# k.v of batches 2 to 7: four 64x64 corners of PE in place of two 64x128 halves

## The chip, the cores and the metric

One core of one Trainium2 chip. The metric is the device time of one execution in microseconds (us). The notes cited as "the Trainium skill" are given with the page's title and section.

Engines: PE (TensorE; PEld is its weight load), DVE (VectorE), ACT (ScalarE), POOL (GpSimd), SP (SyncE).

## The reference

Linear attention on 8 batches of 8 heads, 576 positions, 64 features, followed by a gated feed-forward block on the 4608 rows of 512 that come out.

```python
def _attn_ref(q, k, v):
    phi = lambda x: np.where(x > 0, x, np.exp(x) - 1.0) + 1.0
    q_p, k_p = (phi(q), phi(k))
    kv = np.einsum('bhsd,bhse->bhde', k_p, v)       # 64 x 64 per head: "k.v"
    z = np.sum(k_p, axis=2)
    num = np.einsum('bhsd,bhde->bhse', q_p, kv)
    den = np.einsum('bhsd,bhd->bhs', q_p, z)[..., None] + 1e-06
    return num / den

def _moe_ref(x, w_gate, w_val, w_out):              # 512 -> 1536 -> 512
    g = x @ w_gate
    return (g * (1.0 / (1.0 + np.exp(-g))) * (x @ w_val)) @ w_out
```

## The kernel before

After a start that handles batches 0 and 1 and the first group of 512 rows (g = 0), a main loop of eight iterations, g = 1 to 8, does the feed-forward block of one further group each on PE. In between it prepares attention for batch g + 1, piece by piece: iteration 1 prepares batch 2, iteration 6 prepares batch 7, iterations 7 and 8 prepare no batch. Below is what the change and the argument touch.

A tile of k or v holds two groups of four heads: the even heads on partitions 0 to 63, the odd heads on partitions 64 to 127. `mm1` multiplies 64 positions of two heads of k (128 columns of weights) by the same two heads of v (2 x 65 columns; column 65 of each head is 1, so that it sums k into z). The two halves of the partitions (`hh`) run side by side on the two row halves of PE, into two PSUM banks. Of each 128x129 result only the two 64x64 blocks on the diagonal and one z column are used; the cross products of one head with the other are waste.

```python
def mm1(b, lp):                                   # k.v of two of the four heads per half
    ...
    W = 2 * D + (b > 1)                           # D = 64
    for j in range(J):                            # J = 9 steps of 64 positions
        for hh in range(2):
            rows = slice(C * hh, C * hh + C)      # C = 64
            if b < 2: vv = v16[b][rows, 2 * lp:2 * lp + 2, D * j:D * j + D]
            else:     vv = vm[b % 2][rows, j, :, :].rearrange("p l c -> p (l c)")[:, 130 * lp:130 * lp + W]
            nc.tensor.matmul(out=kvb[b][hh][:, 256 * lp:256 * lp + W],
                             lhsT=kp[b % 2][rows, j, P * lp:P * lp + P], rhs=vv,
                             start=(j == 0), stop=(j == J - 1))

def zdiag(b, lp):                                 # DVE: zd = diagonal matrix of z
    ... nc.vector.tensor_scalar(out=zd[...], in0=id16, scalar1=kvb[b][hh][:, 256 * lp + D:...], ...)

def zb(b):                                        # PE: broadcasts z to all partitions
    nc.tensor.matmul(out=zps[b], lhsT=ones, rhs=zd, start=True, stop=True)

def steady(b, late=0):                            # (n, f): f is issued after the n-th gate pair
    ... (0, phi_q(b, 0)), (1, phi_q(b, 1)), (1, mm1(b, 0)), (1, mm1(b, 1)),
        (2, zdiag(b, 0)), (2, zdiag(b, 1)), (2, r_copies(b)),
        (3 + (late > 0), zb(b)), (3 + (late > 0), zb_copy(b)), (3 + (late > 0), s3_prod(b, 0)),
        (4, s3_reduce(b, 0)), ... (11, s3_recip(b, 2))
```

A "gate pair" n is eight 128x512 matmuls (four into a bank pG, four into a bank pV), then on ACT `sil` = silu of pG, then on DVE `hT` = pV x sil. Iteration 1 is called with `late=2`: all its items come two gate pairs later, and zb one more. In the traces each engine starts this work in program order, so the order of the items is the order on each engine.

## Time and profile before

| | before |
|---|---|
| time, median of the first 4 runs | 331.31 us (330.93 to 331.93) |
| span of the profiled run | 329.4 us |
| PE busy | 317.2 us, 96% |
| k.v of one batch, last full matmul before to first after | 1.44 us |
| iterations 1 to 6, in us | 33.09, 33.36, 33.35, 33.35, 33.32, 33.50 |

An iteration is counted from its first gate matmul to the next one's, in the trace.

The page of the kernel before: busy time by engine, then the granted clock of PE in 40 slices (in tenths of full speed), then the engines' shares in the chain that ended last.

```profile
PE 317.2 (96%) x1957; PEld 150.0 (46%) x1957; DVE 220.0 (67%) x398; ACT 167.6 (51%) x239; POOL 40.5 (12%) x50
...
PEclk9969999999999999999999999999999999999999
...
PE 82%; ACT 5%; DVE 5%; issue 3%; DMA 2%; POOL 1%; SPq 0%; ACTq 0%; POOLq 0%; DVEq 0%
```

PE is busy nearly always, and a first reading is that any PE time saved is time won. The timeline of PE in iteration 2 says otherwise. Columns: start in us, duration in us, engine, line, operation, tiles and shapes.

```profile
98.08 0.38 PE L275 MATMUL pV_115<-xT_0_96,wv 128*128 128x512 f16 x1
98.39 0.23 PE L165 MATMUL pX_118<-vm_76,kp_72 64*128 64x129 f16 x1
98.40 0.23 PE L165 MATMUL pX_119<-vm_76,kp_72 64*128 64x129 f16 x1
98.46 0.22 PE L165 MATMUL pX_118<-vm_76,kp_72 64*128 64x129 f16 x1
98.46 0.22 PE L165 MATMUL pX_119<-vm_76,kp_72 64*128 64x129 f16 x1
...
99.37 0.22 PE L165 MATMUL pX_119<-vm_76,kp_72 64*128 64x129 f16 x1
99.52 0.39 PE L275 MATMUL pG_112<-xT_0_90,wg 128*128 128x512 f16 x1
...
102.77 0.38 PE L275 MATMUL pV_114<-xT_0_96,wv 128*128 128x512 f16 x1
103.16 0.38 PE L195 MATMUL pX_117<-zd,ones 128*128 128x512 f16 x1
```

L165 is k.v: 18 pairs, one pair per 56 ns. L195 is zb. Full matmuls normally start 0.216 us apart, but zb starts 0.386 us after the one before it: it waited 0.17 us, although the durations overlap and PE looks busy. A wait this short does not show as idle time; it shows as a distance between starts. In iterations 2 to 6 that distance is 386, 374, 374, 341 and 523 ns.

What zb waits for is the last zd on DVE. The chain of waits of the kernel before, between 230 and 237 us (iteration 6): start in us, length in us, what.

```profile
230.23 0.10 DVE hT_98 L281
230.33 0.51 issue
230.84 0.46 DVE eq L125
...
233.75 1.12 DVE qp_74 L127 x2
234.87 0.40 issue
235.27 0.69 DVE hT_98 L281
235.96 0.68 DVE zd L171 x4
236.64 0.04 issue
236.68 0.38 PE pX_117 L195
```

The chain to zb runs along DVE: three hT and the phi of q in between, then four zd. k.v is not in it. ("issue" is time in which the engine waited for nothing that the profile shows.)

### The profile page before, as it was taken

The page shows a single profiled execution, that of the slowest core. Times are in us where ns is not written, and L with a number is a line of the kernel's source. Part 1 is how long each engine was busy: PE and PEld are TensorE (multiplying, and loading weights), DVE is VectorE, ACT ScalarE, POOL GpSimd, SP SyncE. Part 2 cuts the span into 40 slices and gives each one's busy share as a digit, 9 for nine tenths or more (in the row PEclk, how much of TensorE's full clock was granted, in tenths as well). Part 3 has the DMA queues.
Part 4 walks back from the last instruction along what each step waited for, and adds up shares of the span by engine and source line. Part 5 has one row for each costly group of instructions (what it writes and reads, how often), then busy time and mean ns, then how long its engine had stood idle before and what let it go on. Part 6 is the DMA issues. An engine that isn't in the chain of part 4 may idle for free.

```text
span 329.4 us, 5083 instructions
## 1 busy us (share of the span) xinstructions
PE 317.2 (96%) x1957; PEld 150.0 (46%) x1957; DVE 220.0 (67%) x398; ACT 167.6 (51%) x239; POOL 40.5 (12%) x50
## 2 busy tenths in 40 slices
PE   8579999999999999999999999999999999999994
PEld 6434454454444444544444444444444444444443
DVE  3855776688978885888588858885887344234321
ACT  3626998927844684458445844584431233123310
POOL 7895410010001000100010000000000000000000
PEclk9969999999999999999999999999999999999999
DMA  7999999999395538363737340224112410140014
GB/s 106 175 125 177 203 207 208 218 225 152 65 159 105 105 80 166 57 115 75 148 71 125 63 100 15 26 54 97 27 24 48 98 32 0 31 91 8 2 32 96
DMA packets 40984, 32.18 MB, mean 98 GB/s; under 512 B 16256, under 2 KB 36480, under 8 KB 40960
## 3 DMA queue, kind: packets, MB, share of 16 engines
q0 software_dynamic: 20640, 18.88, 37.1%
q1 hardware_dynamic: 20160, 12.85, 17.8%
q8 instruction: 15, 0.25, 0.3%
q10 hardware_dynamic: 160, 0.13, 0.2%
q14 instruction: 9, 0.07, 0.1%
HBM read 37.75 MB, written 9.44 MB: 143 GB/s over the span
## 4 chain that ended last, share of the span: by engine, by line
PE 82%; ACT 5%; DVE 5%; issue 3%; DMA 2%; POOL 1%; SPq 0%; ACTq 0%; POOLq 0%; DVEq 0%
PE pG_112 L275 13%; PE pG_113 L275 12%; PE pV_114 L275 8%; PE pV_115 L275 8%; PE pV_116 L275 8%; PE pV_115 L296 7%; PE pG_112 L296 7%; PE pV_114 L296 7%; PE pG_113 L296 6%; DMA q_0_65<-in_q_dram 2%; PE pX_118 L165 2%; DVE hT_98 L281 1%; DVE kp_71 L365 1%; ACT ek L121 1%; ACT sil_100 L280 1%
## 5 line engine op out<-in xcount | busy, mean ns | idle before, releaser
L275 PEld LDWEIGHTS <-wv 128*128 128x128 f16 x432 | 42.5, 98 | 51.6 <-issue 1.1
L275 PEld LDWEIGHTS <-wg 128*128 128x128 f16 x432 | 41.4, 98 | 50.7 <-issue 2.1
L280 ACT ACTIVATE sil_100<-pG_112 128x512 f16<-128x512 f32 x51 | 30.5, 597 | 51.7 <-PE pG_112 L275 45.6
L280 ACT ACTIVATE sil_101<-pG_113 128x512 f16<-128x512 f32 x51 | 30.5, 597 | 37.8 <-PE pG_113 L275 35.1
L296 PEld LDWEIGHTS <-hT_98 128*128 128x128 f16 x228 | 21.4, 98 | 26.0 <-issue 1.5
L296 PEld LDWEIGHTS <-hT_99 128*128 128x128 f16 x192 | 18.4, 98 | 22.8 <-issue 0.9
L306 DVE TENSOR_SCALAR osb_104<-pV_115 128x512 f32<-128x512 f32 x9 | 6.2, 689 | 16.8 <-PE pV_115 L296 16.8
L215 DVE TENSOR_REDUCE den<-prod 128x12 f32<-128x768 f16 x18 | 17.0, 943 | 0.0
L296 PE MATMUL pV_114<-wo,hT_98 128*128 128x512 f16 x60 | 14.1, 379 | 0.2 <-DVE hT_98 L281 0.2
L296 PE MATMUL pV_115<-wo,hT_98 128*128 128x512 f16 x60 | 14.1, 379 | 0.0
L296 PE MATMUL pG_112<-wo,hT_98 128*128 128x512 f16 x60 | 14.1, 379 | 0.0
L281 DVE SCALAR_TENSOR_TENSOR hT_98<-pV_114,sil_100 128x512 f16<-128x512 f32 x11 | 7.6, 691 | 8.4 <-PE pV_114 L275 6.3
L304 ACT ACTIVATE osb_103<-pG_112 128x512 f32<-128x512 f32 x8 | 4.7, 584 | 16.3 <-PE pG_112 L296 16.3
L306 DVE TENSOR_SCALAR osb_105<-pG_113 128x512 f32<-128x512 f32 x8 | 5.5, 691 | 9.4 <-PE pG_113 L296 9.4
L296 PE MATMUL pG_113<-wo,hT_98 128*128 128x512 f16 x48 | 11.4, 380 | 0.0
L296 PE MATMUL pG_113<-wo,hT_99 128*128 128x512 f16 x48 | 11.1, 380 | 0.0
L296 PE MATMUL pV_114<-wo,hT_99 128*128 128x512 f16 x48 | 11.0, 379 | 0.0
L296 PE MATMUL pG_112<-wo,hT_99 128*128 128x512 f16 x48 | 11.0, 379 | 0.0
L296 PE MATMUL pV_115<-wo,hT_99 128*128 128x512 f16 x48 | 11.0, 379 | 0.0
L275 PE MATMUL pG_113<-xT_0_90,wg 128*128 128x512 f16 x27 | 10.5, 388 | 0.0
L275 PE MATMUL pG_113<-xT_0_92,wg 128*128 128x512 f16 x27 | 10.5, 388 | 0.0
L275 PE MATMUL pG_112<-xT_0_90,wg 128*128 128x512 f16 x27 | 10.5, 388 | 0.0
(240 smaller groups left out, 745.2 us busy)
## 6 DMA issues: line engine op xcount, KB each, us to landing
k_1_64<-in_k_dram POOLq DMA_DIRECT2D x4, 576.0 KB, 7.3
q_1_66<-in_q_dram POOLq DMA_DIRECT2D x4, 576.0 KB, 9.4
v_1_68<-in_v_dram POOLq DMA_DIRECT2D x4, 576.0 KB, 11.5
out_dram<-osb_102 SPq DMA_DIRECT2D x18, 128.0 KB, 2.4
out_dram<-osb_103 SPq DMA_DIRECT2D x18, 128.0 KB, 2.4
out_dram<-osb_104 SPq DMA_DIRECT2D x18, 128.0 KB, 2.4
out_dram<-osb_105 SPq DMA_DIRECT2D x16, 128.0 KB, 2.6
k_0_63<-in_k_dram POOLq DMA_DIRECT2D x3, 576.0 KB, 15.8
```

Source lines behind the costliest of these rows:

```text
L121: nc.scalar.activation(out=e[:, s, :], in_=src[b % 2][:, s, :], func=AF.Exp, bias=0.0, scale=1.0)
L165: nc.tensor.matmul(out=kvb[b][hh][:, 256 * lp:256 * lp + W], lhsT=kp[b % 2][rows, j, P * lp:P * lp + P], rhs=vv, start=(j == 0), stop=(j = ...
L215: nc.vector.tensor_reduce(out=den[:, HL * j0:HL * j1], in_=prod[:, 0:j1 - j0, :].rearrange("p j (l d) -> p (j l) d", d=D), axis=AX.X, op=A ...
L275: nc.tensor.matmul(out=ps[:, :], lhsT=src[:, i, P * fb:P * fb + P], rhs=xT[i][g % 2][:, :], start=(i == 0), stop=(i == 3))
L280: nc.scalar.activation(out=s[:, :], in_=pg[:, :], func=AF.Silu, bias=0.0, scale=1.0)
L281: nc.vector.scalar_tensor_tensor(out=hT[g % 2][:, fb, :], in0=pv[:, :], scalar=SC, in1=s[:, :], op0=ALU.mult, op1=ALU.mult)
L296: nc.tensor.matmul(out=pso[(g, t)][:, :], lhsT=hT[g % 2][:, fb, P * t:P * t + P], rhs=wo[:, fb, :], start=(fb == 0), stop=(fb == FB - 1))
L304: nc.scalar.activation(out=o[:, :], in_=ps[:, :], func=AF.Copy, bias=0.0, scale=1.0 / SC)
L306: nc.vector.tensor_scalar(out=o[:, :], in0=ps[:, :], scalar1=1.0 / SC, scalar2=None, op0=ALU.mult)
L365: eng.tensor_scalar(out=dst[:, :, P * lp:P * lp + P].rearrange("p j (s d) -> p s j d", d=D), in0=src[:, 2 * lp:2 * lp + 2, :].rearrange("p ...
```

## The change

The intent is to compute only what is used: one head per 64x64 corner of PE, four corners at once, 65 columns instead of 129. The useless cross products go, and the copy of the result to R reads and writes half as much.

```diff
-    R = two([P, 4, P + 1], FP16, "R")
+    R = two([P, 4, P], FP16, "R")
 ...  def mm1(b, lp):
-                if b < 2: ...  else: vv = vm[b % 2][rows, j, :, :]...[:, 130 * lp:130 * lp + W]
-                nc.tensor.matmul(out=kvb[b][hh][:, 256 * lp:256 * lp + W], lhsT=kp[b % 2][rows, j, P * lp:P * lp + P],
-                                 rhs=vv, start=(j == 0), stop=(j == J - 1))
+                if b < 2: ...  (as before); continue
+                for e in range(2):
+                    nc.tensor.matmul(
+                        out=kvb[b][hh][D * e:D * e + D, 256 * lp:256 * lp + D + 1],
+                        lhsT=kp[b % 2][rows, j, P * lp + D * e:P * lp + D * e + D],
+                        rhs=vm[b % 2][rows, j, 2 * lp + e, :], start=(j == 0), stop=(j == J - 1))
 ...  def r_copies(b):
-        W = 2 * D + (b > 1)
+        W = D
 ...  def kv(b):
-        c1 = D + (b > 1)
+        c1 = D if b < 2 else 0
```

More of the change, by code (lines that the diff above doesn't have):

```diff
@@ L161, in mm1 @@
                 if b < 2:
-                    vv = v16[b][rows, 2 * lp:2 * lp + 2, D * j:D * j + D]
-                else:
-                    vv = vm[b % 2][rows, j, :, :].rearrange("p l c -> p (l c)")[:, 130 * lp:130 * lp + W]
-                nc.tensor.matmul(
-                    out=kvb[b][hh][:, 256 * lp:256 * lp + W], lhsT=kp[b % 2][rows, j, P * lp:P * lp + P], rhs=vv,
-                    start=(j == 0), stop=(j == J - 1))
+                    nc.tensor.matmul(
+                        out=kvb[b][hh][:, 256 * lp:256 * lp + P], lhsT=kp[b % 2][rows, j, P * lp:P * lp + P],
+                        rhs=v16[b][rows, 2 * lp:2 * lp + 2, D * j:D * j + D], start=(j == 0), stop=(j == J - 1))
+                    continue
+                for e in range(2):
+                    nc.tensor.matmul(
+                        out=kvb[b][hh][D * e:D * e + D, 256 * lp:256 * lp + D + 1],
+                        lhsT=kp[b % 2][rows, j, P * lp + D * e:P * lp + D * e + D],
+                        rhs=vm[b % 2][rows, j, 2 * lp + e, :], start=(j == 0), stop=(j == J - 1))
     def zdiag(b, lp):
@@ L175, in r_copies @@
     def r_copies(b):
-        W = 2 * D + (b > 1)
+        W = D
         for hh in range(2):
```

## The prediction

> **What bounds the kernel.** The page gives PE 317.2 of 329.4 us busy (96%); the chain of waits is 82% PE, mostly 128x512 matmuls, one per 0.216 us in the timeline. But PE is not the limit everywhere. In iterations 2 to 6 of the main loop (they prepare batches 3 to 7) the matmul that broadcasts z ("zb", ones x zd) starts late: in the timeline 386, 374, 374, 341 and 523 ns after the matmul before it, against a normal 216. It waits for DVE, which from the iteration's first hT to the last zd runs without a pause (iteration 2: 96.84 to 103.10). The chain of waits for the last such block (230.2 to 236.7 us) runs along DVE, not PE.
>
> **What k.v costs now.** One batch: 18 pairs of row halves, a pair per 56 ns (129 columns), 1.02 us; from the last full matmul before to the first after, 1.44 us (98.08 to 99.52), of which 0.31 is the way into the tiled mode and 0.15 the way out. Six batches.
>
> **What the change does.** 72 matmuls of 64x64 on 65 columns, 18 quartets of corners per batch; twice the instructions. From the trace: pairs on 64 columns (z sums of batch 1, 48.1 to 48.6 us) start every 29 ns. In the existing corner matmuls four start within 10 ns, and a quartet on 64 columns follows another after 28 ns when queued behind longer work (258.97, 259.00), 52 ns when fresh (26.56, 26.62). The Trainium skill, "TensorEngine Tiling (Array Packing)", Restrictions and Gotchas, says that column tiling excludes Fast Weight Load; the trace agrees in kind: 64x64 loads take 103 to 108 ns, 64x128 ones 92 to 95. The 28 ns quartet shows that the slower load still hides. So 52 + 16 x 29 = about 0.52 us for the run: the block shrinks from 1.44 to about 0.96 us. Estimate: 0.48 us less PE time per batch, 2.9 us in all. The copies of kv to R shrink from 258 to 128 columns on ACT (0.39 to about 0.28 us each, estimate from the 512-column evictions at 0.597); ACT is off the chain.
>
> **How much is on the critical path.** k.v lies between the DVE chain's start and zb in iterations 2 to 6. zd there waits not for k.v but for DVE work queued ahead. So PE arrives 0.48 us earlier at zb and waits 0.48 us longer: nothing gained. Only batch 2 (iteration 1), whose zb comes later in the order and waits for nothing (no gap at 75.08), keeps its 0.48 us.
>
> **Predicted: 330.8 us** (331.3 less 0.5), 330.1 to 331.6. Faster by over 2%: 1%; within 2%: 98%; slower by over 2%: 1%.
>
> **What would show it.** Quartets every 29 to 30 ns; the block 1.44 to 0.96 us; the gap before zb grows by 0.48 us in iterations 2 to 6 (to 0.80 to 1.0 us between starts); DVE time from first hT to last zd unchanged at 6.3 to 6.4 us; the iteration that prepares batch 2 0.5 us shorter, the next five unchanged.
>
> **What would make it wrong.** If instructions can't be fed at 8 per 29 ns (the fastest run in the trace is 4 per 29), quartets take up to 56 ns and the gain is nil. If the four weight loads share one port, a quartet costs about 107 ns and the kernel loses up to 5 us, still under 2%. If the DVE chain itself is released by something that moves with k.v, up to 2.9 us are gained (328.4).

## The result, and the profile after

The changed kernel took 330.19 us (median of 4 runs, 329.67 to 330.44), against 331.31 us (median of 4, 330.93 to 331.93). The ratio is 0.9962, with a 95% interval of 0.9943 to 0.9982. A ratio here is the mean time of one kernel's runs over that of the other's of the same rounds, so it is not quite the ratio of the medians that are quoted. The medians differ by 1.1 us, twice the 0.5 that was forecast. Two later comparisons gave 330.19 against 330.94 us (ratio 0.9983) and 330.38 against 331.40 us (0.9978).

The page after, the same lines:

```profile
PE 314.4 (96%) x2173; PEld 147.6 (45%) x2173; DVE 219.2 (67%) x398; ACT 166.3 (51%) x239; POOL 40.5 (12%) x50
...
PEclk9959999999999999999999999999999999999999
...
PE 75%; DVE 11%; ACT 5%; issue 4%; DMA 3%; POOL 1%; SPq 0%; DVEq 0%; POOLq 0%; ACTq 0%
```

PE lost 2.8 us of busy time, but the span only 1.1 us (329.4 to 328.3). DVE's share of the chain rose from 5% to 11%. The timeline of PE in iteration 2, after (instructions of one kind are merged):

```profile
97.54 0.78 PE L166 MATMUL pX<-vm,kp 64*64 64x65 f16 x72
98.26 1.04 PE L276 MATMUL pG<-xT,wg 128*128 128x512 f16 x4
...
102.31 0.38 PE L196 MATMUL pX<-zd,ones 128*128 128x512 f16 x1 [0.43 <-DVE zd L173]
```

The block, from the full matmul before (97.235) to the first after (98.256), now takes 1.02 us. In exchange the wait for zd now shows as idle time, 0.43 us. Start to start before zb it is 806 ns, where it was 386.

Iteration by iteration, from the two traces:

| | 1 | 2 | 3 | 4 | 5 | 6 | sum |
|---|---|---|---|---|---|---|---|
| before, us | 33.086 | 33.364 | 33.352 | 33.351 | 33.320 | 33.504 | 199.98 |
| after, us | 32.667 | 33.365 | 33.354 | 33.353 | 33.317 | 33.324 | 199.38 |
| distance to zb before / after, ns | 216 / 215 | 386 / 806 | 374 / 794 | 374 / 795 | 341 / 758 | 523 / 761 | |

In iteration 1 zb follows the matmul before it without a wait, before the change and after it:

```profile
74.86 0.38 PE L275 MATMUL pV_114<-xT_1_97,wv 128*128 128x512 f16 x1
75.08 0.38 PE L195 MATMUL pX_117<-zd,ones 128*128 128x512 f16 x1
...
73.37 1.03 PE L276 MATMUL pV<-xT,wv 128*128 128x512 f16 x4
74.23 0.38 PE L196 MATMUL pX<-zd,ones 128*128 128x512 f16 x1
```

So the loop gained 0.42 us in iteration 1, nothing in 2 to 5, and 0.18 us in iteration 6: 0.60 us. Of the other 0.45 us of the span, 0.43 were gained before the loop, in code that the change does not touch: its first iteration began at 61.76 us before and at 61.33 us after.

### The profile page after: what moved, and what is told of

It reads as the page before. It is cut to its first block, busy times and chain, and to the rows that moved or that the text cites. A ratio compares the mean times of both kernels' runs of the same rounds, so it can differ in the third digit from the quotient of the medians.

```text
span 328.3 us, 5515 instructions
## 1 busy us (share of the span) xinstructions
PE 314.4 (96%) x2173; PEld 147.6 (45%) x2173; DVE 219.2 (67%) x398; ACT 166.3 (51%) x239; POOL 40.5 (12%) x50
## 4 chain that ended last, share of the span: by engine, by line
PE 75%; DVE 11%; ACT 5%; issue 4%; DMA 3%; POOL 1%; SPq 0%; DVEq 0%; POOLq 0%; ACTq 0%
PE pV L276 22%; PE pG L276 22%; PE pV L297 13%; PE pG L297 13%; DVE qp L127 3%; DVE hT L282 3%; DMA q<-in_q_dram 2%; PE pX L248 1%; DVE eq L125 1%; ACT sil L281 1%; DVE zd L173 1%; DVE kp L366 1%; ACT ek L121 1%; ACT L281 1%; POOL kp L378 1%
## 5 line engine op out<-in xcount | busy, mean ns | idle before, releaser
L276 PE MATMUL pV<-xT,wv 128*128 128x512 f16 x420 | 108.7, 381 | 0.0
L276 PE MATMUL pG<-xT,wg 128*128 128x512 f16 x408 | 106.0, 381 | 0.0
L282 DVE SCALAR_TENSOR_TENSOR hT<-pV,sil 128x512 f16<-128x512 f32 x105 | 72.1, 690 | 50.1 <-PE pV L276 39.3
L281 ACT ACTIVATE sil<-pG 128x512 f16<-128x512 f32 x102 | 60.5, 597 | 88.1 <-PE pG L276 79.3
L297 PEld LDWEIGHTS <-hT 128*128 128x128 f16 x420 | 39.8, 98 | 48.7 <-issue 2.4
L297 PE MATMUL pV<-wo,hT 128*128 128x512 f16 x216 | 50.2, 379 | 0.2 <-DVE hT L282 0.2
L297 PE MATMUL pG<-wo,hT 128*128 128x512 f16 x204 | 47.6, 380 | 0.0
L127 DVE SCALAR_TENSOR_TENSOR kp<-k,ek 128x576 f16<-128x576 f16 x24 | 17.1, 755 | 0.4
L127 DVE SCALAR_TENSOR_TENSOR qp<-q,eq 128x576 f16<-128x576 f16 x24 | 17.1, 755 | 0.4
L229 DVE TENSOR_TENSOR qp<-qp,rden 128x768 f16<-128x768 f16 x18 | 17.1, 951 | 0.2
```

Source lines behind the costliest of these rows:

```text
L127: nc.vector.scalar_tensor_tensor(out=dst[b % 2][:, :, D * l:D * l + D], in0=src[b % 2][:, l, :].rearrange("p (j d) -> p j d", d=D), scalar ...
L229: nc.vector.tensor_tensor(out=qv, in0=qv, in1=rden[:, HL * j0:HL * j1].unsqueeze(2).to_broadcast([P, HL * (j1 - j0), D]), op=ALU.mult)
L276: nc.tensor.matmul(out=ps[:, :], lhsT=src[:, i, P * fb:P * fb + P], rhs=xT[i][g % 2][:, :], start=(i == 0), stop=(i == 3))
L281: nc.scalar.activation(out=s[:, :], in_=pg[:, :], func=AF.Silu, bias=0.0, scale=1.0)
L282: nc.vector.scalar_tensor_tensor(out=hT[g % 2][:, fb, :], in0=pv[:, :], scalar=SC, in1=s[:, :], op0=ALU.mult, op1=ALU.mult)
L297: nc.tensor.matmul(out=pso[(g, t)][:, :], lhsT=hT[g % 2][:, fb, P * t:P * t + P], rhs=wo[:, fb, :], start=(fb == 0), stop=(fb == FB - 1))
```

## The experiments

Theory A is the prediction's: PE time saved before zb is swallowed by the wait at zb, except in iteration 1; what was measured beyond that is chance in the start and one stray delay of DVE in iteration 6. Theory B: the change makes the start and iteration 6 faster for good, by the layout of memory or of the program. Theory C: batches 3 to 7 carry part of the gain. Kernels of one group ran on one chip and share the runs of the kernel before.

### Both kernels again: before_again and after_again

No edit.

> The kernel before, unchanged. Theory A (the change is worth 0.42 us in iteration 1, and the rest of the 1.1 us is the place where the half-clock stretch of the start ends, plus one stray DVE delay of 0.18 us in iteration 6): ratio to itself 1.000 within 0.2%; its trace may start the main loop anywhere from 61.2 to 61.9 us, and iteration 6 should take about 33.3 us, not 33.50. Theory B (the change makes the start and iteration 6 faster for good, by the layout of memory or of the program): the main loop starts at 61.76 again, within 0.05, and iteration 6 takes 33.50 again.

> The changed kernel, unchanged. Theory A: 0.4 to 0.6 us faster than before in paired rounds (ratio 0.9982 to 0.9988), with the start of the main loop as scattered as that of before. Theory B: 1.0 to 1.2 us faster again (ratio 0.9964 to 0.9970), main loop started at 61.33 within 0.05.

Measured: before against itself 0.9995 (0.9975 to 1.0014); the loop began at 61.07 us in this trace, 0.69 earlier than in the first one. The changed kernel: 330.19 against 330.94 us, ratio 0.9983 (0.9963 to 1.0002); its loop began at 62.41 us, 1.08 later than in its first trace. The start is thus scattered by more than the whole effect in either kernel, and theory B's claim about the start falls. (At 61.07 us it also lies outside the 61.2 to 61.9 that was expected.)

But iteration 6 took 33.505 us again, with 522 ns before zb, and 33.319 us again in the changed kernel. Here theory A was wrong: the 0.18 us are not a stray delay. They come back in every trace that has the old halves for batch 7, but for the one where zb moves (before_zb4) and the one where DVE's stream is shifted (before_shift7), both below.

### The change for batch 2 alone, and for batches 3 to 7 alone: only_b2 and only_b3to7

```diff
+    def corner(b):
+        return b == 2          # only_b2;   b > 2 in only_b3to7
-                if b < 2:
+                if not corner(b):   # the old halves
```

R keeps its 129 columns in both.

> Corners for batch 2 alone, batches 3 to 7 as before. Theory A: iteration 1 takes 32.67 us and the gaps before zb of iterations 2 to 6 stay at about 0.37 us; time as the changed kernel, within 0.2 us. Theory C (batches 3 to 7 carry part of the gain): slower than the changed kernel by 0.5 us or more.

> Corners for batches 3 to 7, batch 2 as before. Theory A: iteration 1 takes 33.09 us, iterations 2 to 6 keep 33.32 to 33.36 us with gaps before zb of 0.76 to 0.81 us; time as before within 0.3 us. Theory C: faster than before by 0.5 us or more.

| | time, us | ratio to before | iteration 1 | 2 to 5 | iteration 6 | sum of 1 to 6 |
|---|---|---|---|---|---|---|
| only_b2 | 330.55 | 0.9983 (0.9961 to 1.0005) | 32.668 | as before | 33.505 | 199.56 |
| only_b3to7 | 330.94 | 0.9999 (0.9980 to 1.0018) | 33.086 | as before | 33.324 | 199.80 |

The whole times can't separate 0.4 from 0.6 us (only_b2 was expected within 0.2 us of the changed kernel, and the medians differ by 0.36), but the traces can. Batch 2 is worth 0.42 us, batches 3 to 6 nothing, with 805, 795, 793 and 759 ns before zb in only_b3to7, and batch 7 is worth 0.18 us. Theory C is right for one batch and 0.18 us, and wrong for its 0.5. As R has 129 columns in both kernels, its width has no part in this either.

### zb one step later: before_zb4 and after_zb4

```diff
-            (3 + (late > 0), zb(b)), (3 + (late > 0), zb_copy(b)), (3 + (late > 0), s3_prod(b, 0)),
+            (4, zb(b)), (4, zb_copy(b)), (4, s3_prod(b, 0)),
```

PE now has eight more full matmuls to do while DVE finishes zd. This is the direct test: if zb swallows the gain, the gain must come back in full once zb no longer waits.

> The kernel before with the broadcast of z (zb, its copy and the first product) one step later in iterations 2 to 6, after the fifth gate pair instead of after the fourth. Theory A (zb waits for DVE and swallows what PE saves before it): the waits before zb vanish (start to start 216 ns) and iterations 2 to 6 get shorter by what the gaps were over 216 ns, 0.17, 0.16, 0.16, 0.12 and 0.31 us: 0.9 us in all, ratio to before 0.997. Rival D (the place of zb is not the limit; the DVE chain after it is): no change, or slower.

> The changed kernel with the same move of zb. Theory A: the 0.42 us per batch now count in all six iterations: 0.42 x 6 + 0.9 = 3.4 us faster than before (ratio about 0.990), against the same move on the kernel before 2.5 us faster; gaps before zb 216 ns. Rival D: as the changed kernel, 0.6 us faster than before.

| | time, us | ratio to before | start to start before zb | iterations 2 to 6 | sum of 1 to 6 |
|---|---|---|---|---|---|
| before | 330.66 | | 341 to 523 ns | 33.32 to 33.50 | 199.98 |
| before_zb4 | 330.41 | 0.9983 (0.9966 to 1.0000) | 216 ns | 33.20 | 199.07 |
| after_zb4 | 327.55 | 0.9899 (0.9883 to 0.9916) | 216 ns | 32.78 | 196.56 |

The timeline of PE of the changed kernel with zb one step later, iteration 2:

```profile
97.18 0.78 PE L166 MATMUL pX<-vm,kp 64*64 64x65 f16 x72
97.89 1.04 PE L276 MATMUL pG<-xT,wg 128*128 128x512 f16 x4
...
102.22 1.03 PE L276 MATMUL pV<-xT,wv 128*128 128x512 f16 x4
103.08 0.38 PE L196 MATMUL pX<-zd,ones 128*128 128x512 f16 x1
103.30 0.38 PE L276 MATMUL pG<-xT,wg 128*128 128x512 f16 x1
```

No wait is left. With the move in place, the corners are worth 199.07 - 196.56 = 2.51 us, which is six times 0.42; without it they are worth 0.60. This shows where the gain went, and rival D falls. For before_zb4 alone the interval of the whole times reaches 1.0000; its gain of 0.91 us is read from the traces. after_zb4 beats both kernels: 3.1 us faster than before by the medians, 3.42 us by the loops of the two traces.

### Iteration 6: before_shift7 and after_shift7

Why does batch 7 gain 0.18 us when batches 3 to 6 gain nothing? The DVE timeline of the kernel before, iteration 6:

```profile
233.27 0.45 DVE L125 TENSOR_SCALAR eq<-eq 128x1152 f16<-128x1152 f16 x1
233.75 1.43 DVE L127 SCALAR_TENSOR_TENSOR qp_74<-q_1_66,eq 128x576 f16<-128x576 f16 x2
235.27 0.69 DVE L281 SCALAR_TENSOR_TENSOR hT_98<-pV_116,sil_100 128x512 f16<-128x512 f32 x1
235.88 0.25 DVE L171 TENSOR_SCALAR zd<-id_110,pX_118 128x128 f16<-128x128 f16 x1
```

The same stretch of the changed kernel:

```profile
232.42 0.45 DVE L125 TENSOR_SCALAR eq<-eq 128x1152 f16<-128x1152 f16 x1
232.91 1.43 DVE L127 SCALAR_TENSOR_TENSOR qp<-q,eq 128x576 f16<-128x576 f16 x2
234.25 0.68 DVE L282 SCALAR_TENSOR_TENSOR hT<-pV,sil 128x512 f16<-128x512 f32 x1
234.85 0.75 DVE L173 TENSOR_SCALAR zd<-id,pX 128x128 f16<-128x128 f16 x4
```

From the start of the two phi instructions (the line "x2") to the third hT it is 1.52 us before and 1.34 after. This hT waits for the third gate pair's values in PSUM, which PE makes right after k.v. In the trace's records of semaphores, DVE passes that wait at 234.850 before, yet hT starts at 235.268, 0.418 us later. Its other input is not the reason: sil ended on ACT at 234.579. At the hT of the loop that find DVE free and sil ready this step takes 0.065 us. (Others start later, one of iteration 1 by 0.41 us in both kernels, but they wait for sil: there it ended at 65.792 and hT started at 65.825.) The second phi instruction had started at 234.423, and where nothing holds it the next instruction starts 0.67 us after such a start; so hT lost 0.18 us. After the change the wait is passed 0.42 us earlier relative to the phi instructions (233.588, where the second of them starts at 233.585), so that a hold of 0.4 us would be over while that one is still computing. Whatever the hold is, the corners hide it. Seven extra DVE instructions ahead of everything test whether it belongs to a place in the instruction stream:

```diff
-    nc.vector.memset(epst[:, :], EPS / SC)
+    for _ in range(8):
+        nc.vector.memset(epst[:, :], EPS / SC)
```

> The kernel before with seven more tiny DVE instructions in the idle start, so that every later DVE instruction stands seven places further on in its stream. In iteration 6 of before, the third hT starts 0.418 us after the PE semaphore that it waits for, against 0.066 us elsewhere. Theory E (that hold sits at a place in the DVE's instruction stream): it moves to another instruction, iteration 6 takes about 33.33 us and the gap before zb there about 340 ns: 0.18 us less. Rival F (it belongs to what this hT does or waits for): iteration 6 stays at 33.50 us with 523 ns.

> The changed kernel with the seven tiny DVE instructions. Where the shift alone already took the hold of 0.418 us away from iteration 6, the corners of batch 7 have nothing left to hide there: iterations 1 to 6 take 199.37 us in sum, as in the changed kernel without the shift, against 199.79 us of the kernel before with the shift, so the corners are worth 0.42 us and not 0.60. If the 0.18 us were the corners' own, the sum would be 199.19 us.

| | iteration 6, us | distance to zb in it | sum of 1 to 6 | time, us | ratio to before |
|---|---|---|---|---|---|
| before | 33.504 | 523 ns | 199.98 | 330.66 | |
| before_shift7 | 33.322 | 341 ns | 199.79 | 330.44 | 0.9990 (0.9970 to 1.0010) |
| after_shift7 | 33.326 | 763 ns | 199.38 | 329.96 | 0.9964 (0.9938 to 0.9991) |

(The last line was timed in a later group of runs, beside 331.40 us of the kernel before.) The stretch of DVE in before_shift7:

```profile
232.60 1.43 DVE L127 SCALAR_TENSOR_TENSOR qp<-q,eq 128x576 f16<-128x576 f16 x2
233.94 0.68 DVE L281 SCALAR_TENSOR_TENSOR hT<-pV,sil 128x512 f16<-128x512 f32 x1
```

It is 1.34 us with the old halves too. Seven idle instructions in the start do to iteration 6 what the corners do, and with both together the corners are worth only 199.79 - 199.38 = 0.41 us. So rival F falls: the hold does not belong to this hT. The traces support theory E's place in the stream. Number the recorded DVE instructions from 0 in order of start, those of its sequencer included. This hT is number 447 in every kernel without the shift. All traces were searched, from number 60 on, for a DVE instruction that started late, after an idle stretch, with no semaphore, PE or ACT to explain it. It was found only at number 447 (0.417 to 0.418 us after its semaphore, in the five traces without the shift that have the old halves for batch 7) and at number 191, 256 earlier (0.424 to 0.439 us, in the three kernels with zb one step later, where another hT stands there); never in the two shifted kernels. In other kernels such a hold may be hidden behind work. What happens at these places (a fetch of instructions is one idea) no run here shows.

### The start: before_warm

```diff
+    warm(12, pX[1])
     z0(0, 1)
 ...
+    warm(6, pX[1])
     num0(0)
     den0(1)
+    warm(13, pG[1])
     mm1(0, 1)
```

> The kernel before with 31 spare matmuls in the PE's idle times between 14 and 20 us of the start, so that PE is busy there. Theory A says that the scatter of whole times comes from the half-clock stretch of the start (17.7 to 24.5, 18.7 to 25.5, 19.6 to 26.4 us in three traces, with the main loop at 61.1, 61.8, 62.4). If so: no clock of 0.5 between 10 and 40 us, the main loop starts at 60.5 us or earlier, the times scatter by less than 0.5 us, iterations 1 to 6 as before. Otherwise the scatter stays at 1 us or more with the clock full.

In the twelve traces without these spare matmuls the loop begins at 60.6 to 62.4 us, and PE has a stretch at half clock that begins between 16.8 and 19.6 us and lasts 6.83 us (3.41 us in one). The Trainium skill, "TensorE: Matmul & The Clock Gate", Part 1, describes a free-running activity window of 3413 ns; one and two such windows fit these lengths. In the eleven traces with the longer stretch, the loop begins later where the stretch begins later (correlation 0.99): 60.61 us with a stretch from 16.83 us, 61.33 with 17.83 (the changed kernel), 61.76 with 18.65 (the kernel before), 62.41 with 19.55. The 0.43 us that the first two traces differ by in the start go with this; a correlation does not show which is the cause. The page of before_warm, the granted clock:

```profile
PEclk9999999999999999999999999999999999999999
```

The half clock is gone from the start of this trace and the loop began at 60.43 us, the earliest of all, with iterations 1 to 6 unchanged (199.98 us). But the times did not get better: 330.84 us, ratio 1.0007 (0.9986 to 1.0028), and they scattered over 2.3 us (330.14 to 332.48). The expectation of less scatter failed. Only the run of 330.14 us is traced, with a mean granted clock of 0.999; the slowest one lists 0.994, so the half clock may have come back in it. But the other five still scatter by 1.1 us. The waits of PE in this run (total us, times, longest) show a next limit at once:

```profile
PE pV L296 <- DMA wo<-in_moe_w_out_dram: 1.5, 1, 1.5
```

PE then waits 1.5 us, until 51.3 us, for weights of the feed-forward block; the trace of only_b2, whose stretch lasts 3.41 us, has such a wait of 1.5 us too. The half clock is thus part of the start's scatter at most; what sets the rest is open, since only one run of each kernel is traced.

### The order of the corners: after_zb4_rows

```diff
-            for hh in range(2): ... for e in range(2):
+            for e in range(2): ... for hh in range(2):
```

> The changed kernel with zb one step later, and the four corners of k.v issued with the row half changing fastest instead of the column half. In the trace of the changed kernel a quartet came every 31.6 ns, not the 29 that was forecast. Theory G (loads of the same rows right behind each other cost the 2 to 3 ns): 29 to 30 ns per quartet, the block 1.02 to about 0.98 us, 0.04 us less in each of six iterations. Rival H (the rate of the instructions or of the array sets it, whatever their order): 31 to 32 ns, block 1.02 us, time as with zb one step later, ratio to before 0.990.

The block took 1.02 us in all six iterations, 327.68 us, ratio 0.9905 (0.9881 to 0.9928). The order makes no difference, so theory G falls. What makes a quartet about 32 ns and not 29 stays open. (The 31.6 ns of the expectation leave out the first two steps; the sixteen steps after the first one, which takes 52 ns, have a mean of 31.9.)

### Once more: after_third

No edit; the changed kernel.

> The changed kernel once more, for the size of the whole difference: the traces of the loop say 0.60 us (0.42 in iteration 1 and 0.18 in iteration 6), ratio 0.9982. A ratio of 0.9966 or lower again would mean that the start gains too.

330.38 against 331.40 us, ratio 0.9978 (0.9957 to 0.9998). The loop's sum is 199.38 us, to the hundredth what it was; it began at 62.38 us. Over all runs the mean is 330.32 us (16 runs of the changed kernel) against 330.99 us (43 of the kernel before): 0.67 us, with a standard error of 0.16 worked out from the scatter of both (0.55 and 0.54 us). Eleven of the 43 ran on a chip on which the changed kernel did not run; without them it is 0.74 us. By comparison, in order, the means differ by 1.25, 0.57 and 0.81 us. That fits the 0.60 us of the traces, given the scatter. The first comparison, four runs of each kernel, was a favourable draw; 0.60 us (ratio 0.9982) is the edge of its interval.

## Why the prediction was right or wrong

- **The main mechanism was right.** Batches 3 to 6 gained nothing because PE waits longer at zb by exactly what k.v saves: 386 to 806 ns and likewise in the others. before_zb4 and after_zb4 show it: with the wait gone, the corners are worth 2.51 us, not 0.60.
- **"Only batch 2 ... keeps its 0.48 us" was mis-sized.** It kept 0.42 us. The forecast of the block was 0.96 us and it is 1.02: from the first to the last start of the 72 it takes 0.585 us, not 0.52. Sixteen quartet steps of 31.9 ns in place of 29 make 0.046 of this; the rest is that the four starts of the last quartet are 23 ns apart. The lone 28 ns quartet in the trace before was a poor guide to a row of 18.
- **"zd there waits not for k.v but for DVE work queued ahead" was the step that failed, in iteration 6.** zd's own queue there holds an hT that waits for the gate pair behind k.v, and that hT stood 0.418 us after its semaphore. The chain of waits showed it as "0.40 issue" and the 523 ns stood out from the other four; both were read, and not asked about. It is worth 0.18 us. This is the danger that the prediction itself named last, "released by something that moves with k.v", come true for one batch. "DVE time from first hT to last zd unchanged at 6.3 to 6.4 us" failed for the same reason: it fell from 6.40 to 6.22 us in iteration 6 (in iterations 2 to 5 it is 6.21 to 6.26 us in both kernels).
- **The sum had no term for the start.** "331.3 less 0.5" takes the start as equal in both kernels. Forecast 0.48; the loop gives 0.42 + 0.18 = 0.60. The first comparison's 1.1 us holds about 0.5 us more. Its traces put 0.43 of it in the start, ahead of any changed instruction, where the loop of one and the same changed kernel began over 1 us apart in two traces (0.69 in the kernel before). That the measured gain was twice the forecast is mostly this draw, and not the corners. The range that was given (330.1 to 331.6) held the median, but a range for a forecast of 0.5 us should have allowed for the start.
- **The copies to R** took 0.272 to 0.277 us against 0.28 forecast, and were off the chain as said.
- **The dangers named came hardly or not.** Eight instructions were fed per 32 ns, no quartet took 56 or 107 ns (the first step took 52), and k.v moved only one start on DVE that counted, by 0.18 us.

## What to carry to other kernels

Time saved on the busiest engine counts only as far as the next point at which that engine waits for another. Look for such points by the distance between starts, since a wait of 0.2 us among pipelined matmuls does not show as idle. When a saving is swallowed there, move the waiting instruction behind more of the engine's own work: here one step in the program order, worth 0.91 us by itself, raised what the corners are worth from 0.60 to 2.51 us, 3.42 us together. And when one of five repeats of a loop is different, ask why before calling the loop understood.

## What the Trainium skill lacked or had wrong

- "TensorE: Matmul & The Clock Gate", "Wait — 56ns, not 53.3ns?", says that start-to-start never drops below about 25 ns. Here that holds only from one matmul of a corner to the next: the 72 corner matmuls of a batch started within 0.59 us, 8 ns each, and members of a fresh quartet 3 to 4 ns apart, which agrees with the 4 ns of its Part 3. The page gives no rate for quartets in a row; here it is about 32 ns on 65 columns, where pairs of halves on 64 columns took 29.
- "TensorEngine Tiling (Array Packing)", Restrictions and Gotchas, says that column tiling excludes Fast Weight Load, with no cost beside it. Here 64x64 loads took 102 to 111 ns against mostly 92 to 96 for 64x128 ones, and most of that was hidden: four such loads and their matmuls passed in about 32 ns.
- The same page, Tiling Modes, Key Properties, says that a change of mode drains PE, with no figure. Here the first tiled matmul started 309 ns after a full one, against 216 without a change, and the first full one 0.13 us after the last corner.
- No page has the hold of 0.42 to 0.44 us between a semaphore and a DVE instruction (0.065 us elsewhere), seen at two places of the stream 256 recorded instructions apart, that went away from its hT when the stream was shifted by seven instructions. If it is a fetch of instructions, which is not shown, it belongs to "Runtime: NRT & Kernel Launch", Instruction fetch mechanics.
